# A gated mix of segment attention and a ReGLU block: one up-weight piece is issued ahead of the transposing load of x, the output weight behind the down weight

## The chip, the cores and the metric

The kernel runs on one core of a Trainium2 chip. A core has five engines, each with its own instruction stream: TensorE (PE in the profile, its weight loads PEld), VectorE (DVE), ScalarE (ACT), GpSimd (POOL) and SyncE (SP, which here only issues transfers). Transfers go through DMA queues. The metric is the device time of one execution in microseconds (us). Before the change it was 270.34 us, the median of three runs (269.13, 270.34 and 272.4).

## The reference

The input x has 2048 rows of 512 numbers (bf16). Two branches are computed of it and mixed row by row:

```python
g = sigmoid((x * gate_w).sum(-1, keepdims=True))
# A: attention in 4 segments of 512 rows, 32 heads of 16 numbers
q, k, v = x @ wq, x @ wk, x @ wv              # split by heads and segments
for s in range(4):
    logits = qs @ ks.T * Dh ** -0.5 + causal mask
    a_dot = softmax(logits) @ vs
    a_mem = (phi(qs) @ M) / (phi(qs) @ z + 1e-06)    # phi(t) = t + 1 if t > 0 else exp(t)
    o = gh * a_mem + (1 - gh) * a_dot                # gh = sigmoid(beta), one for each head
    M, z = M + phi(ks).T @ vs, z + phi(ks).sum(rows)
a = o @ wo
# B: a gated block with 1792 inner columns
b = (relu(x @ W_gate) * (x @ W_up)) @ W_down
return g * a + (1 - g) * b
```

Attention is causal within a segment, and a memory (M, z) of the earlier segments is carried along. `wo` is the output weight; `W_gate`, `W_up` and `W_down` are the gate, up and down weights.

## The kernel before

All weights are loaded to SBUF once and stay there: `wq_sb`, `wk_sb`, `wv_sb`, `wo_sb` (512 by 512 each, 512 KB), `wg_sb` and `wu_sb` (512 by 1792) and `wd_sb` (1792 by 512, 1792 KB). The gate and up weights come in four pieces of columns each, numbered 0 to 3: 0 to 255, 256 to 767, 768 to 1279 and 1280 to 1791 (`FP`, line 358). A piece with 512 columns has 512 KB. The 1792 inner columns are worked on in 14 blocks of 128; piece 1 of the up weight holds blocks 2 to 5, and `piece` (line 380) tells which piece a block needs.

The 2048 rows are four segments of 512. For each segment the kernel needs x transposed (`xT`, two buffers that take turns). Segment 0 is loaded plainly and transposed by TensorE. Segments 1 to 3 are loaded by a DMA that transposes on its way (`load_xT`, issued in line 352), one for each segment. Its first readers for segment 1 are projections to v (line 533).

For each segment the work is: the projections to q, k and v (`project`: line 491 for q and k, line 516 or 533 for v); attention in four units of eight heads (`attend`): scores into the PSUM tile `sp` (line 738), the exponential into `E` on ScalarE (749), the causal mask on GpSimd (759), the product with v (808), then a chain on VectorE that starts with a stream transpose into `tA` (826); the memory (`memory`): phi(k) into `pkT` (VectorE, 636), a transposing DMA from `pkT` to `pK` (again line 352) for each of four parts of 128 columns, and the product with v (650); and the gated block (`ffn`): gate and up products (918), relu (930 on ScalarE, 932 on VectorE), product of both into `hT` (937), the down product (952), the output product of attention added in the same PSUM buffer (965), the scaled result (974, 976) and its store (979). Four PSUM buffers `rb` of 128 by 512 serve nearly everything but the scores; a group of matmuls takes one, and the instruction that reads it out gives it back.

The order of instructions on all engines is laid out on the host before anything is emitted. Each piece of work is a `Step` with estimated costs, the steps that it needs (`after`), a due time (`prio`) and a function `emit`. `Plan.lay_out` plays the steps through and picks, for each engine that is free, the waiting step with the least due time; `NUDGE` shifts the due time of every step by a number found beforehand. SP's transfers take part as steps on a queue called `QSP`. The steps are then emitted in the order that came out, and that is each engine's instruction order. Waits are semaphores; a transfer also waits until the eighth transfer before it has landed, since eight semaphores take turns over the transfers.

SP's order for the first 33 us, as it comes out, is: x, `wv`, `wk` and `wq` pieces; gate piece 0; the output weight; up piece 0; three gate and two up pieces; the transposing load of x of segment 1; the two loads of `Vs` (parts of v shifted to the other half of the partitions, line 464); two of the four transposes into `pK`; up piece 1; the other two transposes into `pK`; the down weight. Among the steps, the loads that the change touches are these (lines 375 to 378 and 414):

```python
    ld[f"wu{n}"] = dma("SP", wu_sb[:, :, a:b], rows(B_W_up, a, b), prio=2 + n, kb=b - a)
ld["wd"] = dma("SP", wd_sb[:], rows(B_W_down), prio=7, kb=1792)
ld["wo"] = dma("SP", wo_sb[:], rows(A_wo), prio=8)
ld_x[1] = load_xT(1, xps, prio=6)
```

Of the kernel before, what the change touches and what calls it, by code (L numbers as in the profile page):

```python
# [225 lines left out]
def kernel(  # L226
# [120 lines left out]
    ld_x, ld = {}, {}  # L347
# [637 lines left out]
    for seg in range(NSEG):  # L985
        project(seg)
        attend(seg)
        if seg < NSEG - 1:
            memory(seg)
            if seg == 0:  # L990
                ld["wd"].after += st[0]["PK"]
        else:
            st[seg]["mz"] = []
        ffn(seg)
        st[seg]["readers_xT"] = st[seg]["xr"]
    plan.makespan = plan.lay_out()
    for s in plan.order:
        s.emit(s.start[2], s)
# [30 lines left out]
```

## Time and profile before

| what | us |
|---|---|
| median of three runs | 270.34 |
| profiled execution, its own time | 270.74 |
| its span, first to last instruction | 269.0 |
| TensorE busy (matmuls) | 263.0 |
| ScalarE busy | 192.3 |
| VectorE busy | 185.3 |
| GpSimd busy | 162.4 |

The profile is of one execution. Its own time is 1.74 us longer than its span, which counts from the first instruction to the last. The share of busy time says which engine is fullest, and not what a wait on another engine costs: this has to be read from the place where the wait stands. A row of the timeline gives start, duration, engine, line, operation, tiles and, in brackets, the engine's idle time just before it with what ended it. SPq rows are the issue of transfers, and their duration is the time in which SP is occupied by the issue, not the transfer itself; the view of DMA gives the time from issue to landing. The granted TensorE clock was 1.00 over the whole span.

### The profile page before, as it was taken

How to read it: one execution, taken by the hardware profiler on the slowest of the kernel's cores; microseconds unless marked ns; L12 is line 12 of the kernel's file. 1: busy time of each engine (PE TensorE's matmuls, PEld its weight loads, DVE VectorE, ACT ScalarE, POOL GpSimd, SP SyncE). 2: the span in 40 equal slices, each digit the busy share in tenths (PEclk: the TensorE clock that was granted, in tenths of full speed). 3: DMA queues.
4: the chain of work that ended last, by engine and by line, in shares of the span. 5: the costliest groups of instructions: out<-in, count | busy, mean ns of one | idle time of the engine just before them, and what ended most of it. 6: DMA issues, size and time to landing. Idle time of an engine off the chain costs nothing.

```text
span 269.0 us, 8042 instructions
## 1 busy us (share of the span) xinstructions
PE 263.0 (98%) x3365; PEld 120.9 (45%) x3365; DVE 185.3 (69%) x414; ACT 192.3 (71%) x185; POOL 162.4 (60%) x378
## 2 busy tenths in 40 slices
PE   8999799999999999999999999999999999999995
PEld 5444344444455444444444544444444444344444
DVE  1477697799489966986767767897826535878800
ACT  3789799987689977777979777765659757876021
POOL 8435767465888874655684888645425685735400
PEclk9999999999999999999999999999999999999999
DMA  6997980420302310000030000000010100000011
GB/s 202 327 347 150 120 273 5 57 66 2 80 2 73 73 43 22 2 2 0 13 68 22 23 19 2 23 4 0 2 45 22 37 5 22 0 4 2 2 39 39
DMA packets 26293, 15.06 MB, mean 56 GB/s; under 512 B 13585, under 2 KB 26257, under 8 KB 26257
## 3 DMA queue, kind: packets, MB, share of 16 engines
q1 hardware_dynamic: 25904, 14.29, 21.1%
q8 instruction: 26, 0.43, 0.7%
q10 hardware_dynamic: 288, 0.26, 0.3%
q14 instruction: 11, 0.08, 0.1%
q0 software_dynamic: 64, 0.00, 0.0%
HBM read 8.13 MB, written 2.10 MB: 38 GB/s over the span
## 4 chain that ended last, share of the span: by engine, by line
PE 94%; DMA 3%; ACT 1%; SPq 1%; DVE 0%; issue 0%; DVEq 0%; ACTq 0%
PE rb L918 37%; PE rb L952 17%; PE rb L491 10%; PE sp L738 9%; PE rb L808 7%; PE rb L965 5%; PE rb L533 3%; DMA wu_sb<-in_B_W_up_dram 2%; PE rb L516 2%; PE rb L876 1%; PE rb L779 1%; DMA xT<-in_A_x_dram 1%; ACT E L749 1%; PE rb L650 1%; PE rb L404 1%; SPq L352 1%
## 5 line engine op out<-in xcount | busy, mean ns | idle before, releaser
L749 ACT ACTIVATE E<-sp 128x2048 bf16<-128x2048 f32 x72 | 135.1, 1876 | 36.2 <-PE sp L738 34.4
L759 POOL TENSOR_SCALAR_AFFINE_SELECT E<-E 64x256 bf16<-64x256 bf16 x256 | 112.9, 441 | 77.3 <-ACT E L749 65.1
L918 PE MATMUL rb<-xT,wu_sb 128*128 128x512 bf16 x224 | 55.9, 380 | 1.5 <-DMA wu_sb<-in_B_W_up_dram 1.5
L918 PE MATMUL rb<-xT,wg_sb 128*128 128x512 bf16 x224 | 55.6, 380 | 0.0
L937 DVE TENSOR_TENSOR hT<-rb,rg 128x512 bf16<-128x512 f32 x56 | 38.1, 683 | 24.7 <-PE rb L918 15.7
L952 PE MATMUL rb<-wd_sb,hT 128*128 128x512 bf16 x210 | 49.2, 380 | 0.0
L918 PEld LDWEIGHTS <-wu_sb 128*128 128x128 bf16 x224 | 20.5, 98 | 26.9 <-issue 3.0
L918 PEld LDWEIGHTS <-wg_sb 128*128 128x128 bf16 x224 | 20.3, 98 | 26.2 <-issue 4.3
L738 PE MATMUL sp<-QT,KT 16*64 16x320 bf16 (+7 forms) x512 | 30.3, 295 | 0.1
L952 PEld LDWEIGHTS <-hT 128*128 128x128 bf16 x210 | 19.3, 98 | 24.6 <-issue 3.5
L738 PE MATMUL sp<-QT,KTo 32*64 32x320 bf16 (+7 forms) x512 | 30.3, 295 | 0.0
L930 ACT ACTIVATE rg<-rb 128x512 bf16<-128x512 f32 x35 | 20.8, 595 | 8.8 <-PE rb L918 7.0
L826 DVE STREAM_TRANSPOSE tA<-rb 128x512 f32<-128x512 f32 x32 | 20.8, 689 | 7.0 <-PE rb L808 7.0
L738 PEld LDWEIGHTS <-KT 16*64 16x64 bf16 x512 | 10.6, 102 | 28.3 <-issue 28.3
L974 ACT ACTIVATE osb<-rb,ngcol 128x512 bf16<-128x512 f32 x11 | 7.5, 685 | 15.9 <-PE rb L965 15.9
L808 PE MATMUL rb<-E,Vs 64*32 64x448 bf16 (+7 forms) x512 | 18.8, 284 | 0.0
L808 PE MATMUL rb<-E,Vp 64*32 64x448 bf16 (+7 forms) x512 | 18.4, 284 | 0.0
L491 PE MATMUL rb<-xT,wq_sb 128*128 128x512 bf16 x64 | 16.3, 380 | 0.0
L491 PE MATMUL rb<-xT,wk_sb 128*128 128x512 bf16 x64 | 16.1, 379 | 0.0
L965 PE MATMUL rb<-wo_sb,oT 128*128 128x512 bf16 x60 | 15.1, 380 | 0.0
L932 DVE TENSOR_SCALAR rg<-rb 128x512 bf16<-128x512 f32 x21 | 14.2, 682 | 1.3 <-PE rb L918 0.7
L389 DVE CAST QT<-rb 128x512 bf16<-128x512 f32 x11 | 7.6, 687 | 9.4 <-PE rb L491 9.4
(107 smaller groups left out, 313.9 us busy)
## 6 DMA issues: line engine op xcount, KB each, us to landing
out_dram<-osb SPq DMA_DIRECT2D x15, 128.0 KB, 1.7
wd_sb<-in_B_W_down_dram SPq DMA_DIRECT2D x1, 1792.0 KB, 7.5
wg_sb<-in_B_W_gate_dram SPq DMA_DIRECT2D x3, 512.0 KB, 7.7
wu_sb<-in_B_W_up_dram SPq DMA_DIRECT2D x3, 512.0 KB, 7.8
Vs<-Vp SPq DMA_DIRECT2D x8, 144.0 KB, 3.4
wk_sb<-in_A_wk_dram SPq DMA_DIRECT2D x2, 256.0 KB, 4.5
wq_sb<-in_A_wq_dram SPq DMA_DIRECT2D x2, 256.0 KB, 5.5
wo_sb<-in_A_wo_dram SPq DMA_DIRECT2D x1, 512.0 KB, 6.8
```

Source lines behind the costliest of these rows:

```text
L491: nc.tensor.matmul(rb[s.bank][:], lhsT=w[:, ci, c * P:(c + 1) * P], rhs=xT[i][:, ci, :], start=(ci == 0), stop=(ci == NC - 1))
L738: nc.tensor.matmul(sp[64 * h:64 * h + 64, j, off:off + m], lhsT=kt[32 * j:hi, c0 + w, 64 * ck:64 * ck + 64], rhs=QT[i][32 * j:hi, c0 + w, ...
L749: nc.scalar.activation(Er[n % NE][:], sp[:], ACT.Exp, scale=SCALE)
L759: nc.gpsimd.affine_select(out=v, in_=v, compare_op=ALU.is_ge, fill=0.0, base=0, pattern=[[0, 4], [1, 64]], channel_multiplier=-1)
L808: nc.tensor.matmul(rb[s.banks[h]][32 * j:32 * j + 32, q0:q0 + m], lhsT=v[64 * h:64 * h + 64, ck // 2, o:o + 32], rhs=Er[(base + f) % NE][6 ...
L826: nc.vector.transpose(tA[k].rearrange("p b w -> p (b w)"), rb[a.banks[r]][:])
L918: nc.tensor.matmul(rb[s.bank][:], lhsT=w[:, ci, fv * P:(fv + 1) * P], rhs=xT[i][:, ci, :], start=(ci == 0), stop=(ci == NC - 1))
L930: nc.scalar.activation(rgb[k][:], rb[a.bank][:], ACT.Relu)
L932: nc.vector.tensor_scalar(rgb[k][:], rb[a.bank][:], 0.0, None, ALU.max)
L937: nc.vector.tensor_tensor(hT[:, fv, :], rb[a.bank][:], rgb[k][:], ALU.mult)
L952: nc.tensor.matmul(rb[b][:], lhsT=hT[:, fv, lc:lc + P], rhs=wd_sb[:, fv, :], start=(fv == 0), stop=False)
L965: nc.tensor.matmul(rb[hold.bank][:], lhsT=oT[i][:, ci, lc:lc + P], rhs=wo_sb[:, ci, :], start=False, stop=(ci == NC - 1))
```

## The change

After all steps are set up and before the order is laid out, a helper moves the issue of two transfers to the places of two others. The step that is moved stays in the plan as it was, with its costs and its due time, but emits nothing; its instruction is emitted with the host step instead. So the plan, and with it the order on all other engines, is the same as before, and only SP's instruction order differs: piece 1 of the up weight is issued directly ahead of the transposing load of x of segment 1, and the output weight directly behind the down weight. The steps that read the two weights wait for the transfers where these stand now.

```diff
         ffn(seg)
         st[seg]["readers_xT"] = st[seg]["xr"]
+
+    def issue_with(step, host, first):
+
+        own, hosts = step.emit, host.emit
+        step.emit = lambda e, s: None
+
+        def both(e, s):
+            for fn in (own, hosts) if first else (hosts, own):
+                fn(e, s)
+        host.emit = both
+    issue_with(ld["wu1"], ld_x[1], True)
+    issue_with(ld["wo"], ld["wd"], False)
     plan.makespan = plan.lay_out()
     for s in plan.order:
         s.emit(s.start[2], s)
```

## The prediction

> **What bounds the kernel now.** I read the page first: the span and the busy time by engine.
>
> ```profile
> span 269.0 us, 8042 instructions
> ...
> PE 263.0 (98%) x3365; PEld 120.9 (45%) x3365; DVE 185.3 (69%) x414; ACT 192.3 (71%) x185; POOL 162.4 (60%) x378
> ```
>
> PE is busy for 263.0 of 269.0 us, every other engine for 71% at most. So the time is the matmuls plus PE's few holes, and the question is where these lie. The view of waits, asked for PE alone, has just three rows:
>
> ```profile
> PE rb L918 <- DMA wu_sb<-in_B_W_up_dram: 1.5, 1, 1.5
> PE rb L394 <- DVE zeros L265: 1.1, 1, 1.1
> PE rb L404 <- DMA xT<-in_A_x_dram: 0.3, 1, 0.3
> ```
>
> The last two belong to the start. The first is a single wait of 1.5 us for a transfer of the up weight. The stages (columns: stretch, its length, PE busy with its count, then the other engines, the granted clock, DMA share, GB/s) place it:
>
> ```profile
> 0.00:25.00 25.00, 23.66 (x185) 11.56 (x185) 12.30 (x38) 17.17 (x27) 14.13 (x35) 1.00 0.94 269
> 25.00:32.00 7.00, 5.52 (x59) 3.35 (x52) 5.20 (x17) 6.26 (x8) 4.45 (x11) 1.00 1.12 130
> 32.00:266.00 234.00, 233.86 (x3131) 106.01 (x3129) 167.40 (x359) 168.87 (x151) 143.80 (x334) 1.00 0.12 31
> ```
>
> From 32 to 266 us PE lacks 0.14 us in 234; from 25 to 32 it lacks 1.48 us in 7, at a clock of 1.00. Whatever reaches PE earlier at 32 us is followed by work that waits for nothing but PE's own order. PE's timeline and, in the second fence, the chain of waits (start, length, what) show the hole itself:
>
> ```profile
> 25.05 1.05 PE L533 MATMUL rb<-wv_sb,xT 128*128 128x257 bf16 x8
> ...
> 31.53 1.04 PE L918 MATMUL rb<-xT,wu_sb 128*128 128x512 bf16 x4 [1.48 <-DMA wu_sb<-in_B_W_up_dram]
> ...
> 39.20 1.04 PE L918 MATMUL rb<-xT,wg_sb 128*128 128x512 bf16 x4
> ```
>
> ```profile
> 25.38 6.11 DMA wu_sb<-in_B_W_up_dram
> ```
>
> PE is done at 31.53 − 1.48 = 30.05 and waits until the piece, issued at 25.38, has landed at 25.38 + 6.11 = 31.49. SP's timeline tells why the issue is so late:
>
> ```profile
> 6.17 0.51 SPq L340 DMA_DIRECT2D wo_sb<-in_A_wo_dram  x1
> ...
> 12.81 1.16 SPq L340 DMA_DIRECT2D wu_sb<-in_B_W_up_dram  x1
> 14.08 7.10 SPq L352 DMA_TRANSPOSE xT<-in_A_x_dram  x1
> ...
> 25.38 0.58 SPq L340 DMA_DIRECT2D wu_sb<-in_B_W_up_dram  x1
> ...
> 28.69 3.46 SPq L352 DMA_TRANSPOSE pK<-pkT  x1
> 32.20 0.57 SPq L340 DMA_DIRECT2D wd_sb<-in_B_W_down_dram  x1
> 45.77 5.73 SPq L352 DMA_TRANSPOSE pK<-pkT  x3
> ```
>
> The piece stands behind the transposing load (7.10 us in issue), two loads of Vs and two pK transposes, while the output weight, 512 KB, takes a place among the first.
>
> **The change, part by part.** On SP the output weight leaves its place after the first gate piece, so the six issues behind it move up by one; the up piece takes the place in front of the transposing load; behind the down weight the output weight comes in. The other engines keep their order. The transfers concerned (KB, us from issue to landing; the pK rows are the transfer issued at 28.69, and the one at 24.07, ahead of the up piece):
>
> ```profile
> xT<-in_A_x_dram SPq DMA_TRANSPOSE x1, 9.1
> wu_sb<-in_B_W_up_dram SPq DMA_DIRECT2D x1, 512.0 KB, 8.5
> wo_sb<-in_A_wo_dram SPq DMA_DIRECT2D x1, 512.0 KB, 6.8
> wd_sb<-in_B_W_down_dram SPq DMA_DIRECT2D x1, 1792.0 KB, 7.5
> pK<-pkT SPq DMA_TRANSPOSE x1, 4.9
> pK<-pkT SPq DMA_TRANSPOSE x1, 2.4
> ```
>
> *The up piece, earlier.* It takes the very place that another up piece of 512 KB has now: issue at 12.81, landing 8.5 us later, at 21.3. That is 8.7 us ahead of 30.05, so the wait of 1.48 us goes: −1.48. Its second condition is an empty PSUM buffer; it writes the one whose last reader is this VectorE row, over at 28.92 + 0.14 = 29.06, a microsecond before 30.05:
>
> ```profile
> 28.92 0.14 DVE L543 TENSOR_SCALAR zg<-rb 128x1 f32<-128x1 f32 x1
> ```
>
> *The transposing load of x.* 512 KB leave the queue in front of it and 512 KB enter, in the same number of issues, so it is issued at 14.08 and lands at 14.08 + 9.1 = 23.2 as now. Its first reader is the PE row at 25.05, 1.85 us later. Cost 0; if the two pieces do not cancel, 1.85 us are the cover.
>
> The Trainium skill bears on this ("DMA: Bandwidth & Descriptors", section Queues, rings and completion order): on each DMA engine descriptors are consumed in ring order, so every byte put ahead of the transposing load delays it, and the trace's order of landings (21.3, then 23.2) agrees. By that rule, if the output weight's removal gave nothing back, 512 KB at the 269 GB/s of the first 25 us would delay the load by an estimated 1.95 us, 0.10 more than the cover, and the sum below would be −1.38.
>
> *The gate and up pieces that move up one place* land earlier; none is waited for now. Gain 0.
>
> *The output weight, later.* Issued after the down weight, it adds one issue of 0.51 us to SP and lands at the latest one whole transfer after it. What stands behind it on SP starts at 45.77. Its first reader (durations, first and last start):
>
> ```profile
> L965 PE MATMUL rb<-wo_sb,oT x60: 379/379/390, 77.9 to 261.6; 128*128 128x512 bf16 x60
> ```
>
> The down weight lands at 32.20 + 7.5 = 39.7, the output weight by 39.7 + 6.8 = 46.5; the cover is 77.9 − 46.5 = 31.4 us. Cost 0.
>
> *The pK transposes behind the old place* lose 512 KB in front of them. This matters, because the next question is what is late once PE runs on. The idle time that the other engines have during the hole:
>
> ```profile
> 32.99 1.88 ACT L749 ACTIVATE E<-sp 128x2048 bf16<-128x2048 f32 x1 [1.69 <-PE sp L738]
> 34.94 0.89 POOL L759 TENSOR_SCALAR_AFFINE_SELECT E<-E 64x256 bf16<-64x256 bf16 x2 [1.32 <-ACT E L749]
> 32.60 0.69 DVE L937 TENSOR_TENSOR hT<-rb,rg 128x512 bf16<-128x512 f32 x1 [1.34 <-PE rb L918]
> 33.70 0.69 DVE L636 SCALAR_TENSOR_TENSOR pkT<-KT,e1k 128x512 bf16<-128x512 bf16 x1 [0.40 <-DMA pK<-pkT]
> 37.66 1.31 DVE L826 STREAM_TRANSPOSE tA<-rb 128x512 f32<-128x512 f32 x2
> ```
>
> ScalarE has 1.69, more than is needed. GpSimd has 1.32, so its masks may come 0.16 late; they serve the second unit of segment 0, whose product with V is 18 us away by the chain of waits:
>
> ```profile
> 53.62 1.10 PE rb L808 x64
> ```
>
> VectorE has 1.34 + 0.40 = 1.74, if its second wait shrinks too: that one is for the pK transfer issued at 28.69, which lands at 28.69 + 4.9 = 33.59. From 33.70 VectorE runs without a hole to the pair of stream transposes at 37.66; the first ends at 37.66 + 1.31/2 = 38.32 and frees the PSUM buffer that PE writes at 39.20. So PE could come 0.88 us earlier there at no more cost; for the whole 1.48 the pK transfer has to land 0.6 us earlier than now. The bounds: landing as now, gain 0.88; landing like its neighbour ahead of the piece, 2.4 us after issue, at 31.1, gain 1.48 with 1.9 us to spare. I take the second, since what stood in front of it is gone.
>
> **Sum.** −1.48 + 0 + 0 + 0. The profiled execution lasts 270.74 us, 1.74 around its span of 269.0; it becomes 269.26, the span 267.5. It lies 0.40 above the median of the three runs, so against the median: 270.34 − 1.48 = 268.86, 0.55% faster. That is less than the 1% that a measurement of this kernel can tell from no change.
>
> **The rivals.**
>
> *The hole is filled only in part* (0.88 instead of 1.48): the pK transfer stays late. For it speaks what DMA did between 28.5 and 32 us (GB/s in 40 slices of 0.0875 us):
>
> ```profile
> GB/s 310 263 243 287 205 243 231 489 152 120 47 23 15 0 0 29 23 0 0 0 0 0 0 0 3 9 6 9 12 9 9 12 9 35 252 263 275 269 20 6
> ```
>
> For 23 slices, 2.0 us, nearly nothing moves, with both transfers outstanding; if what holds the piece now then holds the pK transfer, VectorE's limit stays. Against it: less is queued. Time 270.34 − 0.88 = 269.5.
>
> *The hole is not there in ordinary executions.* Without those 2.0 us of standstill the piece would land at 31.49 − 2.0 = 29.5, before 30.05, and nothing would be gained: 270.3. For it: the three times differ by 3.27 us (269.13 to 272.4), more than the whole gain. Against it: the program is the same in every execution, so the gap should fall in the same place; that is argued, no row shows it.
>
> *Slower: the transposing load lands late.* If the piece in front of it costs it the 6.11 us that the piece takes now, it lands at 23.2 + 6.11 = 29.3, and PE waits at 25.05 for 4.25 us; less the 1.48 won, that is 2.77 slower, 273.1. It decides from a delay of 1.85 + 1.48 = 3.33 us on. Against it: the up piece now in the same place, with equal bytes before it, lands 1.9 us ahead of the load. For it: nothing but the 7.10 us that this load already spends in issue.
>
> The Trainium skill ("TensorE: Matmul & The Clock Gate", Part 1: The HAM clock gate) says that a PE idle for a window of about 3.4 us falls to half speed for about as long again; a stall of 4.25 us could then cost an estimated 1.7 us more, 274.8. The present hole of 1.48 us shows no such fall, the clock is 1.00; no row here shows a longer one.
>
> *The change does not do what it says*: SP's order would have to be otherwise. It is as described, so this has no chance of its own.
>
> **How the numbers follow.** Forecast 268.9: 0.65. Filled in part, 269.5: 0.13. No hole in ordinary runs, 270.3: 0.15. Late load, 273.1: 0.05. Something unforeseen: 0.02. The upper end is no gain plus a little, 270.6; the lower is the forecast less half the spread of the three runs, 1.6: 267.3. Beyond 1%, below 267.6, only scatter leads, or a hole larger in other executions than in this one: 0.14. Slower, above 273.0: the late load and the unforeseen, 0.06. Within 1%: 0.80.
>
> **What would show it.** In the profile after, PE's waits have no row for the up weight, and PE lacks under 0.2 us from 25 to 32. SP issues the up piece at about 12.8 and the transposing load at about 14.1, which lands near 23.2; the group at 25.05 waits for nothing. The pK transfer issued at 28.7 lands before 33.0. The output weight lands before 47. PE's last matmul ends 1.5 us earlier, and the span is 267.5. It is wrong if a new PE wait stands between 25 and 40 us (for xT, or for VectorE at the group now at 39.20), if the pK transfer still lands at 33.6, or if PE's busy time itself grows.

## The result, and the profile after

The changed kernel takes 268.91 us in the median of 12 runs (268.17 to 269.32). The kernel before took 270.35 in 12 runs beside it (268.78 to 272.41). The ratio is 0.9939, with a 95% interval of 0.9913 to 0.9965, which leaves out 1: 0.6% faster, as forecast (268.9). The two spreads differ too: 3.63 us before, 1.15 after. The profiled execution of the changed kernel lasts 268.84 us; its clock is 1.00 over the whole span.

The page of the changed kernel, span and busy time:

```profile
span 267.1 us, 8000 instructions
...
PE 258.6 (97%) x3322; PEld 120.8 (45%) x3365; DVE 185.4 (69%) x414; ACT 192.3 (72%) x185; POOL 163.5 (61%) x378
```

PE's busy time seems to fall by 4.4 us, but the page counts 3322 matmuls where there are 3365 weight loads: 43 records are missing, and so is their time. This matters for the view of PE's waits after the change (total, count, longest):

```profile
PE rb L952 <- issue: 1.4, 9, 0.2
PE rb L394 <- DVE zeros L265: 1.1, 1, 1.1
PE rb L404 <- DMA xT<-in_A_x_dram: 0.5, 1, 0.5
PE rb L965 <- issue: 0.5, 3, 0.2
PE rb L918 <- issue: 0.3, 2, 0.2
```

The rows that name "issue" are new, each at most 0.2 us long, about the time of one matmul (a group of four lasts 1.04 us), and they come with the missing records; they are no waits. The run with the up piece alone, further below, bears this out: its profile has all 3365 matmuls and no such row, and takes equally long behind the change. The row "L918 <- DMA wu_sb" with its 1.5 us is gone, and nothing takes its place. The stages of the changed kernel (columns as in the prediction):

```profile
25.00:32.00 7.00, 6.95 (x64) 3.92 (x64) 5.75 (x18) 6.93 (x9) 4.43 (x11) 1.00 0.45 69
32.00:266.00 234.00, 228.42 (x3077) 105.33 (x3114) 167.12 (x359) 167.94 (x151) 144.69 (x333) 1.00 0.12 33
```

From 25 to 32 us PE now lacks 0.05 us instead of 1.48. In the second stage (32 to 266 us) the missing records make the busy time useless, so the comparison goes by starts. First the one row of the kernel before that the prediction did not need, PE's last group ahead of the hole (the last part of the projection to v for segment 1), and behind it PE's timeline of the changed kernel:

```profile
29.45 0.60 PE L533 MATMUL rb<-wv_sb,xT 128*128 128x256 bf16 x4
```

```profile
24.79 1.05 PE L533 MATMUL rb<-wv_sb,xT 128*128 128x257 bf16 x8
...
29.18 0.60 PE L533 MATMUL rb<-wv_sb,xT 128*128 128x256 bf16 x4
29.62 1.02 PE L918 MATMUL rb<-xT,wu_sb 128*128 128x512 bf16 x4
...
37.28 1.04 PE L918 MATMUL rb<-xT,wg_sb 128*128 128x512 bf16 x4
```

From that last group to the up product it was 31.53 − 29.45 = 2.08 us, and now it is 29.62 − 29.18 = 0.44: 1.64 less. Of this, 1.48 is the hole in brackets; the other 0.16 is there because groups that follow each other overlap in PE's pipeline (0.44 from start to start, with a group that lasts 0.60), which the bracket does not count. The group at 39.20 comes 1.92 earlier, and the span is 1.9 shorter. What is left, 0.27 us, stands ahead of the change: the first groups for segment 1 start at 24.79 instead of 25.05. That difference is there at 6.6 us already (the matmul of line 418 starts at 6.59, before at 6.85), and SP's first differing issue is at 6.16, so no moved transfer can have caused it. It is scatter of the start.

SP's timeline of the changed kernel, and in the second fence its transfers (KB, us from issue to landing, in this order: the up piece, issued at 11.71, the transposing load, the fourth pK transfer, issued at 28.42, and the output weight):

```profile
10.82 2.58 SPq L340 DMA_DIRECT2D wu_sb<-in_B_W_up_dram  x2
13.52 7.05 SPq L352 DMA_TRANSPOSE xT<-in_A_x_dram  x1
22.14 7.82 SPq L352 DMA_TRANSPOSE pK<-pkT  x4
30.01 0.58 SPq L340 DMA_DIRECT2D wd_sb<-in_B_W_down_dram  x1
30.64 0.90 SPq L340 DMA_DIRECT2D wo_sb<-in_A_wo_dram  x1
```

```profile
wu_sb<-in_B_W_up_dram SPq DMA_DIRECT2D x1, 512.0 KB, 9.0
xT<-in_A_x_dram SPq DMA_TRANSPOSE x1, 9.0
pK<-pkT SPq DMA_TRANSPOSE x1, 3.3
wo_sb<-in_A_wo_dram SPq DMA_DIRECT2D x1, 512.0 KB, 8.8
```

The up piece lands at 20.7, 8.9 us ahead of its reader at 29.62. The transposing load lands at 13.52 + 9.0 = 22.5, 2.2 us ahead of its reader. All four pK transfers go out in one row, since nothing stands between them any more; the fourth lands at 31.7 instead of 33.59. The output weight lands at 39.5.

VectorE, which the prediction named as the engine that could be late next (timeline of the changed kernel):

```profile
30.92 0.67 DVE L937 TENSOR_TENSOR hT<-rb,rg 128x512 bf16<-128x512 f32 x1
31.82 0.69 DVE L636 SCALAR_TENSOR_TENSOR pkT<-KT,e1k 128x512 bf16<-128x512 bf16 x1 [0.23 <-DMA pK<-pkT]
...
35.97 1.30 DVE L826 STREAM_TRANSPOSE tA<-rb 128x512 f32<-128x512 f32 x2
```

Its 1.34 us of idle time ahead of L937 is gone, and of the 0.40 ahead of L636 there is 0.23 left. The stream transposes start 1.69 earlier.

### The profile page after: what moved, and what is told of

It is laid out like the page before. It is cut to its first block, busy times and chain, and to the rows that moved or that the text cites. A ratio compares the mean times of both kernels' runs of the same rounds, so it can differ in the third digit from the quotient of the medians.

```text
span 267.1 us, 8000 instructions
## 1 busy us (share of the span) xinstructions
PE 258.6 (97%) x3322; PEld 120.8 (45%) x3365; DVE 185.4 (69%) x414; ACT 192.3 (72%) x185; POOL 163.5 (61%) x378
## 4 chain that ended last, share of the span: by engine, by line
PE 92%; issue 2%; POOL 2%; DMA 1%; ACT 1%; DVE 1%; SPq 0%; DVEq 0%; POOLq 0%
PE rb L918 36%; PE rb L952 16%; PE rb L491 10%; PE sp L738 9%; PE rb L808 7%; PE rb L965 5%; PE rb L533 4%; DMA wv_sb<-in_A_wv_dram 1%; PE rb L876 1%; PE rb L779 1%; PE rb L516 1%; POOL E L759 1%; ACT E L749 1%; POOL mnum L668 1%; DVE tA L826 0%
## 5 line engine op out<-in xcount | busy, mean ns | idle before, releaser
L918 PE MATMUL rb<-xT,wg_sb 128*128 128x512 bf16 x214 | 55.0, 380 | 0.6
L918 PE MATMUL rb<-xT,wu_sb 128*128 128x512 bf16 x212 | 54.7, 380 | 0.8 <-issue 0.3
L937 DVE TENSOR_TENSOR hT<-rb,rg 128x512 bf16<-128x512 f32 x56 | 38.1, 684 | 23.3 <-PE rb L918 14.6
L952 PE MATMUL rb<-wd_sb,hT 128*128 128x512 bf16 x198 | 47.0, 379 | 1.6 <-issue 1.4
L918 PEld LDWEIGHTS <-wg_sb 128*128 128x128 bf16 x224 | 20.4, 98 | 26.2 <-issue 4.3
L918 PEld LDWEIGHTS <-wu_sb 128*128 128x128 bf16 x224 | 20.6, 98 | 25.2 <-issue 3.0
L808 PE MATMUL rb<-E,Vs 64*32 64x448 bf16 (+7 forms) x512 | 18.8, 284 | 0.0
L808 PE MATMUL rb<-E,Vp 64*32 64x448 bf16 (+7 forms) x512 | 18.4, 284 | 0.0
L965 PE MATMUL rb<-wo_sb,oT 128*128 128x512 bf16 x57 | 14.4, 379 | 0.5 <-issue 0.5
L389 DVE CAST QT<-rb 128x512 bf16<-128x512 f32 x11 | 7.6, 689 | 9.4 <-PE rb L491 9.4
```

What stands on the lines that cost most here:

```text
L808: nc.tensor.matmul(rb[s.banks[h]][32 * j:32 * j + 32, q0:q0 + m], lhsT=v[64 * h:64 * h + 64, ck // 2, o:o + 32], rhs=Er[(base + f) % NE][6 ...
L918: nc.tensor.matmul(rb[s.bank][:], lhsT=w[:, ci, fv * P:(fv + 1) * P], rhs=xT[i][:, ci, :], start=(ci == 0), stop=(ci == NC - 1))
L937: nc.vector.tensor_tensor(hT[:, fv, :], rb[a.bank][:], rgb[k][:], ALU.mult)
L952: nc.tensor.matmul(rb[b][:], lhsT=hT[:, fv, lc:lc + P], rhs=wd_sb[:, fv, :], start=(fv == 0), stop=False)
L965: nc.tensor.matmul(rb[hold.bank][:], lhsT=oT[i][:, ci, lc:lc + P], rhs=wo_sb[:, ci, :], start=False, stop=(ci == NC - 1))
```

## The experiments

Three things are to be told apart: whether the hole is in every execution (rival b), what the fourth pK transfer costs when it is late (rival a), and what a late transposing load costs (rival c). Beside that: which half of the change does the work.

One measure serves for all runs, because the start scatters by some tenths: the **rest**, from the start of PE's last group of the projection to v for segment 1 (29.45 before, 29.18 after) to the end of the span. All in us; "pK4" is the landing of the fourth pK transfer, counted from that same start, and the wait is PE's longest behind 15 us.

| kernel | time of the profiled execution | rest | pK4 | PE's wait |
|---|---|---|---|---|
| before | 270.74 | 239.57 | 4.15 | 1.48, up piece |
| before, second profile | 269.61 | 238.97 | 2.61 | 0.86, up piece |
| before, third profile | 270.36 | 239.66 | 4.21 | 1.57, up piece |
| changed | 268.84 | 237.94 | 2.54 | none |
| changed, second profile | 269.18 | 237.93 | 2.79 | none |
| up piece alone | 268.82 | 237.91 | 2.90 | none |
| output weight alone | 268.58 | 237.92 | 3.34 | none |
| the two exchanged | 268.43 | 237.91 | 2.92 | none |
| exchanged, second profile | 268.52 | 237.94 | 2.88 | none |
| exchanged, third profile | 269.00 | 237.94 | 3.22 | none |
| exchanged, fourth profile | 269.44 | 238.44 | 3.88 | 0.32, VectorE |
| pK transfers late | 273.79 | 242.70 | 6.78 | 3.22, VectorE |
| transposing load late | 273.48 | 237.91 | 1.99 | 3.09, load of x (ahead of the rest) |

Every profile without a wait in this part has a rest of 237.91 to 237.94, so a difference of some hundredths is readable here, where the times themselves scatter by several tenths.

### One half of the change at a time

The up piece alone: the output weight stays where it was, so 512 KB more stand ahead of the transposing load.

```diff
     issue_with(ld["wu1"], ld_x[1], True)
-    issue_with(ld["wo"], ld["wd"], False)
```

> Only the up piece is moved ahead of the transposing load of x; the output weight keeps its early place, so 512 KB more stand in front of that load. Theory (PE's hole was the whole cost, the load has a cover of 1.85 us): the piece lands at about 22.5, the load 1.4 to 1.95 us later than in the kernel before, at 24.6 to 25.1, the group at 25.05 waits at most 0.1 us, and nearly the whole gain stays: ratio 0.994 to 0.995. Rival (the output weight's removal is what gains): the load is late by more than 2 us, PE waits there, ratio 1.00 or above.

Measured: 268.85 us (268.5 to 269.22), ratio to before 0.9946 (0.9926 to 0.9966). SP's timeline, the transfer and its reader on PE, in this run:

```profile
16.03 6.49 SPq L352 DMA_TRANSPOSE xT<-in_A_x_dram  x1
```

```profile
xT<-in_A_x_dram SPq DMA_TRANSPOSE x1, 8.5
```

```profile
24.77 1.05 PE L533 MATMUL rb<-wv_sb,xT 128*128 128x257 bf16 x8
```

The load lands at 16.03 + 8.5 = 24.5, 2.0 us later than in the changed kernel and 0.25 us ahead of its reader. So the output weight's removal gives back 2.0 us, and without it nearly the whole cover is used up, yet nothing is lost. Against the kernel before, where the load lands at 23.2, the up piece in front costs it 1.3 us. So for this load the change's two halves cancel, as the prediction had it, with some tenths to spare in these profiles.

The output weight alone: the up piece stays between the pK transfers.

```diff
-    issue_with(ld["wu1"], ld_x[1], True)
     issue_with(ld["wo"], ld["wd"], False)
```

> Only the output weight is moved behind the down weight; the up piece keeps its place behind the pK transposes. Theory: everything behind the output weight on SP comes about 1.4 us earlier, the piece is issued at 24.0 instead of 25.38; if it then takes 6.1 us as before it lands at 30.1 and the hole is all but gone (ratio 0.994 to 0.996); if instead the standstill of the transfers between 29 and 31 us sets its landing, it lands at 31.4 as before and nothing is gained (ratio 0.999 to 1.001). The trace's landing tells the two apart.

Measured: 268.9 us (268.58 to 269.24), ratio 0.9958 (0.9934 to 0.9981). SP's timeline and the transfer:

```profile
23.41 0.58 SPq L340 DMA_DIRECT2D wu_sb<-in_B_W_up_dram  x1
```

```profile
wu_sb<-in_B_W_up_dram SPq DMA_DIRECT2D x1, 512.0 KB, 3.9
```

The piece is issued 2.0 us earlier than before and lands at 27.3, 4.2 us earlier, because it takes 3.9 us instead of 6.1: it is through before the stretch of 2.0 us (29.4 to 31.4 in the kernel before) in which next to nothing moved. Neither of the two landings that I had expected, 30.1 and 31.4, came about: the duration shrank as well. So either half alone fills the hole, one by taking the piece out of the row, the other by taking 512 KB out of what stands ahead of it. The intervals of the halves and of the whole overlap; no version beats the changed kernel by what these runs can tell.

### Is the hole in every execution?

The kernel before, profiled twice more with no edit.

> The kernel before, unchanged, profiled once more: does the hole vary between executions? Theory A (the hole is fixed by the order of issue): 1.3 to 1.6 us again, landing of the up piece 6.0 to 6.2 us after its issue. Theory B (it hangs on how long the transfers stand still, which varies): the hole and the landing differ, and the time of the execution follows the hole one to one: about 268.9 plus the hole.

> A third profile of the kernel before, as above: A: hole 1.3 to 1.6 us; B: another hole, time about 268.9 plus the hole.

PE's timeline, of the second profile and then of the third:

```profile
28.90 0.60 PE L533 MATMUL rb<-wv_sb,xT 128*128 128x256 bf16 x4
...
30.36 1.04 PE L918 MATMUL rb<-xT,wu_sb 128*128 128x512 bf16 x4 [0.86 <-DMA wu_sb<-in_B_W_up_dram]
```

```profile
28.99 0.60 PE L533 MATMUL rb<-wv_sb,xT 128*128 128x256 bf16 x4
...
31.16 1.04 PE L918 MATMUL rb<-xT,wu_sb 128*128 128x512 bf16 x4 [1.57 <-DMA wu_sb<-in_B_W_up_dram]
```

The hole is 0.86, 1.48 or 1.57 us, with one and the same program: theory B. The rest over 237.93 is 1.04, 1.64 and 1.73: each time the hole and 0.16 to 0.18 for the pipeline that has to fill again. Subtracted from the times, that gives 268.57, 269.10 and 268.63, which is where the executions of the changed kernel lie. Taking the hole out halves the spread of these three, from 1.13 to 0.53 us; what is left is no more than the changed kernel's own. The slowest executions of the kernel before, at 272.4, were not profiled, and the largest hole that was seen does not reach that far. There is a hint at what they are: of the 32 executions of the kernel before that were run beside the experiments, the slowest, at 272.74, had a mean granted clock of 0.994, and all others had 0.998 or more. A clock of 0.994 is what most executions with a PE wait of about 3 us show further below. Over a span of 271.0 us it is an estimated 1.6 us, which would leave about 2.2 us of the excess over 268.9 for the hole itself; no profile shows this.

What varies is the landing. Instruction fetches show in the view of DMA between 28 and 32 us (queue, packets, MB, share of 16 engines), in the first profile of the kernel before and in the second:

```profile
q14 instruction: 1, 0.01, 3.9%
```

```profile
q14 instruction: 1, 0.01, 0.5%
```

A share of 3.9% of 16 engines over 4 us is one DMA engine for 2.5 us; 0.5% is 0.3 us. The third profile, with the hole of 1.57, has 4.0%. So in these three, long fetches and late landings go together. In the four profiles of the exchanged kernel (next part) they do not: the one with a wait has 3.7% and the others 0.9 to 1.1%, but in one of the latter, with 1.0%, the transfer in the up piece's old place lands 2.11 us after PE's last projection row, as late as in the third profile of the kernel before (2.12). A long fetch is not needed for a late landing, then; whether it ever causes one these runs do not tell, and the cause of the standstill stays open. The Trainium skill ("Runtime: NRT & Kernel Launch", Instruction fetch mechanics) says that each engine's sequencer fetches its instructions in blocks of 16 KiB over a DMA queue of its own, and that the cost is mostly hidden. By the page of the kernel before, the packets of queue 8 have about that size (26 for 0.43 MB) and those of queue 14 about half of it (11 for 0.08 MB); no row here names a wait for one of them.

### The fourth pK transfer and VectorE

The two transfers exchanged: the up piece goes to the output weight's early place, and the output weight between the pK transfers, so that 512 KB stay ahead of the fourth.

```diff
-    issue_with(ld["wu1"], ld_x[1], True)
-    issue_with(ld["wo"], ld["wd"], False)
+    ld["wu1"].emit, ld["wo"].emit = ld["wo"].emit, ld["wu1"].emit
```

> The two transfers change places: the up piece early, where the output weight was, and the output weight between the pK transposes, where the up piece was. PE's hole is gone, but 512 KB stand in front of the third and fourth pK transposes again. My theory of what is late next: the fourth lands near 33.6 as before, VectorE waits for it, PE gets a wait on VectorE of about 0.6 us at the group at 39.2 (then about 38.3), and the gain is 0.88 us (ratio 0.9965 to 0.997). Rival: VectorE does not limit, the gain is 1.4 to 1.6 us as in the changed kernel (ratio 0.994).

> The exchange of the two places profiled once more, since its profiled execution was the fastest of its twelve (268.43 us, the median 269.40) and its fourth pK transfer had landed at 31.7. Theory: in an execution near the median that transfer lands at 32.7 or later, VectorE waits longer than 1 us for it, and PE has a wait on VectorE of 0.5 us or more near 38 us. Rival: no wait of PE on VectorE at all, the spread comes from elsewhere.

Measured: 269.4 us (268.43 to 270.0), ratio 0.9969 (0.9946 to 0.9993). The median is the one that VectorE's limit would give, but the profiled execution, at 268.43 the quickest of all, shows no wait, nor does the second profile. In both the fourth pK transfer lands at 31.7 and not near 33.6; pK4 is 2.92 and 2.88. That proves nothing either way, so the same wait was made large: all of the down weight and the output weight, 2304 KB, go between the second and the third pK transfer, into the up piece's old place.

```diff
     issue_with(ld["wu1"], ld_x[1], True)
     issue_with(ld["wo"], ld["wd"], False)
+    issue_with(ld["wd"], ld["wu1"], True)
```

> As the changed kernel, but the down weight and the output weight (2304 KB) stand between the second and the third pK transpose, where the up piece was in the kernel before, so that the fourth pK transfer is late for certain. At 356 GB/s the two take 6.6 us, so it lands at 33.5 to 34.7 instead of 31.7. Theory (VectorE is what is late next): VectorE waits for it at the second pkT, PE has 0.66 us of slack there in the changed kernel and loses the rest: waits of PE on VectorE of 1.1 to 2.5 us between 33 and 39 us, time 270.0 to 271.4 us. Rival (VectorE makes it good behind its dense stretch, or PE does not depend on it): no wait of PE between 33 and 40 us, time 268.9.

Measured: 274.37 us (273.79 to 275.59), ratio 1.0174 (1.0133 to 1.0215). VectorE's timeline, PE's, and the stages around the wait (columns as before, the granted clock third from the end):

```profile
36.26 0.69 DVE L636 SCALAR_TENSOR_TENSOR pkT<-KT,e1k 128x512 bf16<-128x512 bf16 x1 [4.46 <-DMA pK<-pkT]
36.87 0.68 DVE L389 CAST QT<-rb 128x512 bf16<-128x512 f32 x1
```

```profile
37.61 0.31 PE L808 MATMUL rb<-E,Vp 64*32 64x64 bf16 x8 [3.22 <-DVE QT L389]
```

```profile
37.00:38.00 1.00, 0.39 (x28) 0.39 (x36) 1.00 (x2) 0.41 (x1) 0.00 (x0) 0.54 0.00 0
38.00:39.00 1.00, 1.00 (x40) 0.65 (x32) 1.00 (x4) 1.00 (x2) 0.00 (x0) 0.50 0.00 0
39.00:40.00 1.00, 1.00 (x17) 0.13 (x2) 1.00 (x2) 0.98 (x1) 0.00 (x0) 0.50 0.06 16
40.00:41.00 1.00, 1.00 (x5) 0.44 (x4) 1.00 (x3) 0.00 (x0) 0.82 (x2) 0.76 0.00 0
```

The chain is readable row by row: the transfer lands at 36.16, VectorE may then write `pkT` again (L636), behind it in VectorE's order stands the cast that reads out a PSUM buffer (L389), and PE's product with v (L808) needs that buffer. PE waits 3.22 us. Of the rest's 242.70 − 237.93 = 4.77 us the wait is 3.22 and the refilling 0.17; 1.38 are left for the clock. The profiled execution, the quickest of its four at 273.79, is 2.4 us beyond the upper end of what was expected. The larger part of that is the clock, which fell to 0.50 and had not been counted; another 0.72 is the wait, 3.22 where at most 2.5 was expected, because the transfer landed about 1.5 us later than allowed for. Not all of this delay counted, since the slack was larger than the 0.66 allowed for (3.56 − 2.54 = 1.02, by the paragraph that follows).

This run also gives the point from which the transfer counts: landing at 6.78 costs a wait of 3.22, so a landing at 6.78 − 3.22 = 3.56 costs none. All profiles of a kernel without a wait lie below (the largest is 3.34). Two more profiles of the exchanged kernel test that number.

> The exchange of the two places once more: both profiled executions so far (268.4 and 268.5 us) lay at the fast end of its times (268.4 to 270.0). Theory: when the transfers stand still for about 2 us between 28 and 31 us, the fourth pK transfer lands more than 3.56 us after the start of PE's last projection to v, and PE waits for VectorE at the product with v (line 808) by what lies beyond that; an execution of 269.4 or more shows this wait, one of 268.5 none. Rival: an execution of 269.4 or more without such a wait.

> The exchange of the two places a fourth time, to catch an execution near its median of 269.40: with a wait of PE on VectorE near 34 us (theory), or at that time without one (rival).

The third profile has pK4 at 3.22 and no wait. The fourth has it at 3.88, above the point by 0.32; VectorE's timeline and PE's:

```profile
33.27 0.69 DVE L636 SCALAR_TENSOR_TENSOR pkT<-KT,e1k 128x512 bf16<-128x512 bf16 x1 [1.56 <-DMA pK<-pkT]
33.88 0.68 DVE L389 CAST QT<-rb 128x512 bf16<-128x512 f32 x1
```

```profile
34.62 0.25 PE L808 MATMUL rb<-E,Vp 64*32 64x64 bf16 x8 [0.32 <-DVE QT L389]
```

PE waits 0.32 us, and its rest is 0.51 longer than without, again the wait and 0.19. So VectorE's limit is there, with the same chain at a tenth of the size, and an execution either meets it or does not, by the landing of one transfer. How often it is met is not shown: only this one execution near the median was profiled. In the kernel before pK4 was 4.15 and 4.21 in two executions of three: by the point of 3.56, a change that filled the hole and left this transfer where it was would have waited 0.59 and 0.65 us there; no run tests this case.

The changed kernel was profiled once more, to see whether it keeps below that point:

> The changed kernel profiled a second time. Theory: no PE wait behind the start again, the fourth pK transfer lands less than 3.56 us after the start of PE's last projection to v, and from that start to the span's end it takes 237.9 us as in the first profile.

Its pK4 is 2.79, its rest 237.93, its time 269.18, with no wait. Both executions stay 0.8 us and more below 3.56.

### A late transposing load

The down weight, 1792 KB, goes ahead of the transposing load too.

```diff
     issue_with(ld["wu1"], ld_x[1], True)
+    issue_with(ld["wd"], ld_x[1], True)
     issue_with(ld["wo"], ld["wd"], False)
```

> As the changed kernel, but the down weight (1792 KB) stands in front of the transposing load of x as well. At 269 to 365 GB/s that is 5.0 to 6.8 us, so the load lands at 27.6 to 29.4 instead of 22.6. Theory (cover 1.85 to 2.2 us, every us beyond it costs PE one): PE waits 2.8 to 4.6 us at the group at 24.8, and the time is that much above the changed kernel's, ratio to the kernel before 1.005 to 1.012. Rival (later work makes it good, since all engines run ahead meanwhile): ratio below 1.003. A second rival: a stall of over 3.4 us lowers the granted clock, and it costs up to 1.7 us more; the clock in the stages behind the stall tells.

Measured: 273.28 us (271.72 to 274.15), ratio 1.0111 (1.0078 to 1.0145). PE's timeline and the stages from 24 us on:

```profile
27.76 1.41 PE L533 MATMUL rb<-wv_sb,xT 128*128 128x257 bf16 x8 [3.09 <-DMA xT<-in_A_x_dram]
...
33.84 0.60 PE L533 MATMUL rb<-wv_sb,xT 128*128 128x256 bf16 x4
```

```profile
24.00:28.00 4.00, 0.91 (x21) 0.37 (x20) 0.74 (x2) 2.55 (x3) 2.46 (x7) 1.00 0.98 156
28.00:29.00 1.00, 1.00 (x9) 0.77 (x7) 0.49 (x2) 0.00 (x0) 0.56 (x2) 0.66 0.95 235
29.00:30.00 1.00, 1.00 (x4) 0.42 (x3) 0.49 (x2) 0.00 (x0) 0.00 (x0) 0.50 0.41 91
30.00:31.00 1.00, 1.00 (x5) 0.41 (x3) 0.69 (x1) 0.08 (x1) 0.00 (x0) 0.50 0.48 107
31.00:32.00 1.00, 1.00 (x8) 0.69 (x6) 0.15 (x1) 0.97 (x2) 0.00 (x0) 0.64 0.04 10
32.00:34.00 2.00, 2.00 (x29) 1.10 (x27) 1.67 (x6) 1.60 (x2) 0.00 (x0) 1.00 0.83 73
```

The load lands at 27.72, 5.16 us later than in the changed kernel, and its reader waits 3.09. In the changed kernel the load was 24.79 − 22.56 = 2.23 ahead of its reader, which leaves 2.93 of the delay; PE also ran dry 0.12 earlier here, at 24.67. So the delay beyond the cover counts in full. But PE's last group of this projection starts at 33.84, 4.66 us later, 1.57 more than the wait. The stages show where these lie: PE is busy throughout from 28 to 32 us, but at a granted clock of 0.66, 0.50, 0.50 and 0.64. Summed, 0.34 + 0.50 + 0.50 + 0.36 = 1.70 us of full-speed work are lost. The rest behind it is 237.91, so nothing of the delay is made good later, and nothing more is lost. The clock did not fall in every execution: six of the seven had a mean granted clock of 0.992 to 0.994 and took 273.01 us or more, and the one with 1.000 took 271.72, which was not profiled.

## Why the prediction was right

*The sum.* The forecast was a gain of 1.48 by the one hole; the medians differ by 1.44. In the profile the term is 1.64, the hole and 0.16 of pipeline that the bracket does not show, and beside it 0.27 of scatter of the start. That the forecast met the median to 0.05 us is partly luck: the execution from which it was worked out had one of the larger holes, but lay 0.4 above the median, and the prediction took the 1.48 off the median. The size depends on which executions one takes, too: the 32 of the kernel before that were run beside the experiments have a median of 269.95, and against these the two halves of the change gain 1.10 and 1.05.

*The up piece* lands 8.9 us early, 8.7 forecast: right. *The transposing load* is issued at 13.52 instead of the 14.1 forecast and lands at 22.5 (23.2): right, and its cover is real, as the runs with one half and with the late load show. *The output weight* lands at 39.5 against a bound of 46.5: right. By the rule on ring order that the prediction took from the Trainium skill ("DMA: Bandwidth & Descriptors", Queues, rings and completion order), with nothing given back for the output weight, the sum would have been −1.38. The run with the up piece alone is that case: its load is issued 1.95 us later than in the kernel before, as estimated, but lands only 1.33 later, 8.5 us after its issue instead of 9.1, and is still 0.25 early. So what stands ahead does delay the load, as the rule has it, but here by less than the estimate, and nothing of the gain was lost.

*What is late next.* The number was right and the place was wrong. The prediction let VectorE's limit bind at the group at 39.20, by way of the stream transposes. It binds earlier, at the product with v, through the cast that stands behind the same L636. The prediction's place is close behind: in the run with the wait of 0.32 that group starts at 37.90, and the first stream transpose ends at about 37.7. The size hardly differs: "0.6 us earlier than now" was the forecast, and 4.15 − 3.56 = 0.59 is what it takes. The value chosen for the landing, 2.4 us after issue by its neighbour's row, was too good; it took 3.3. The bound at which the gain shrinks was 33.0, and it landed at 31.7, so the wrong value cost nothing. With the landing of before, the gain would have been 1.64 − 0.59 − 0.17 = 0.88, which is the prediction's lower bound, to be sure by another way of working it out.

*Filled in part* (rival a) is not what this change does, in two profiles of two. It is a mechanism of this kernel all the same: the exchanged kernel meets it in one profile of four, and its median of 269.4 is close to the 269.5 given.

*No hole in ordinary executions* (rival b) was wrong as put, and so was the argument against it. The hole is in all three profiles, but "the same program, so the same place" is refuted: it goes from 0.86 to 1.57. The spread of the times, which the prediction listed for this rival, was a sign of a gap that moves, though not of that alone.

*The late load* (rival c) does not happen here. Its price of one for one beyond the cover is right (a wait of 3.09, where delay and cover leave 2.93 and the start another 0.12), but its time was too low, since a wait of that size also lowers the clock: with the wait alone it would be 268.9 + 3.09 = 272.0, and measured were 273.28. The rule of the Trainium skill that the prediction weighed beside it ("TensorE: Matmul & The Clock Gate", Part 1: The HAM clock gate) made an estimated 1.7 us of it; 1.57 beyond the wait were measured. So the rival belonged at the higher of its two times, in six executions of seven, though the fall came at a shorter wait than the window of about 3.4 us that the Trainium skill gives there.

## What to carry to other kernels

Where one engine is busy for 98% of the span, its single hole is worth its own length and a little more (here 0.16 to 0.19 us for the pipeline to fill), provided that the engine which would be late next is looked up beforehand: follow each of the others through the hole and note which of its waits ends when. A late transfer is moved not only by its own place, but by every one ahead of it in the same queue; either edit alone filled this hole. And a gap that hangs on a landing differs from execution to execution, so a kernel whose times spread by more than its neighbour's may show in its spread part of what the single profile shows as a hole.

## What the runs showed of the hardware

- A PE wait of 3.09 us and one of 3.22 us each brought one stretch at half clock; the waits of up to 1.57 us in the profiles of the kernel before did not. Taking the clock as either 1.00 or 0.50, the four stages with the late load put the stretch at 28.32 to 31.72, those with the late pK transfers at 37.08 to 40.48: 3.40 us both times. It began 3.65 us after PE had run dry in the first (0.56 after PE was at work again) and 2.69 us after it in the second (PE still idle), so the moment is not fixed by the wait alone. The Trainium skill ("TensorE: Matmul & The Clock Gate", Part 1: The HAM clock gate) speaks of a free-running window of 3413 ns; the length agrees, and the two waits show that PE need not be idle for a whole window.
- The same 512 KB transfer, in the same place of the same program, landed 2.03, 1.42 and 2.12 us after the same PE row. What holds the queue up for about 2 us behind 28 us is not settled.
- The start of the span scatters by some tenths (29.45, 28.90 and 28.99 for the same PE row of the kernel before), which is as much as the changes in question; a measure that begins at a row behind the start and ahead of the change is steady to 0.03 us.
